# Attention and mixture of experts in one kernel: the gate's places, the masks and the first pair's halves at other steps, and the last batch's token list beside the second layer

## The chip, the cores and the metric

One core of a Trainium2 chip runs the whole kernel. The metric is the device time of one launch in microseconds, lower is better; several runs of one kernel are shown by their median.

## The reference, cut to what matters

Clustered attention feeds a mixture of experts. B, H, S, D are 4, 8, 768, 64; there are 16 clusters, 3072 tokens of width 512, 8 experts with a hidden width of 1024, and each token goes to 2 experts.

```python
q_assign = argmax(einsum('bhsd,hcd->bhsc', q_n, c_n)); k_assign = the same of k_n
mask = q_assign[..., :, None] == k_assign[..., None, :]
attn = softmax(where(mask, q @ k.T / sqrt(D), -1e9))
x = (attn @ v) as [B * S, H * D]
noisy = x @ w_gate + log1p(exp(x @ w_noise)) * noise
two best experts of each token, weights by softmax over the two
out[token] += weight * (relu(x[token] @ w1[e]) @ w2[e])      # for both experts e
```

## The kernel before

**Pairs and steps.** The attention goes over 16 pairs of heads, 4 pairs to a batch, 12 steps to a pair. In step t TensorE (PE) computes the scores of one block of 128 keys (`scores`, L547), ScalarE (ACT) takes their exponent (L548), and a step later GpSimd (POOL) splits it into two halves of 16 bits (`split_p`, L559; VectorE (DVE) does it for the last pairs). Four steps later PE multiplies them by v (`values`, L580, L582, L586), and DVE divides by the sums (L591 to L594).

**The list of steps.** All else is put by hand on thirds of steps with `at(step, function)`: a step has three slots, ahead of its scores, behind them, and behind the values. The slots fix each engine's order of instructions and the order of SP's queue, which issues nearly all DMAs; every engine works through its own order and waits where something is missing. What is put on one slot runs in the order in which the loop over the pairs put it there. In the loop `w = 12 * (p - 2)` is a pair's origin, `z = w + 36 + L` (L is 4) that of a finished batch's gate; at the end of the list `z` is 192, the last step of the attention.

**A pair's preparation.** q and k are transposed and split (`a_split`), placed into the tiles A and B by DMA (`b_place`), and compared with the centroids (`a_sims`, `a_sum`, `a_max1` to `a_eq`). `a_mask` transposes the one-hot rows on PE (L480), which waits for DVE's `oh` (L471), ACT writes them to `mk`, and `b_mask` puts them into A by four DMAs (L488). Then `b_max` finds each row's largest score: 12 times two matmuls (L516) and two DVE reductions, one of which goes to the PSUM tile `aux` (L519). `b_neg` (L526 to L528) and `b_negT` (L533) turn the result, and a DMA puts it into B (`B<-nt`).

**v.** `load_v` fills the one tile `vt`; `v_split` reads it head by head (ACT L402, L403; POOL L404). The next `load_v` waits in SP's queue until the last head was split.

**A finished pair.** `x_hi` (ACT L645) and `x_lo` (POOL L649) split its output into `xh`, `x_put` (L654) writes this to DRAM, `x_turn` (L661) transposes it by DMA into `xt`.

**A batch's gate.** `g_halves` (L681) multiplies the four turned pairs by the gate's weights, `g_turn` (L708, L713) turns the logits. `g_gate` makes a list of small operations, nearly all on DVE over 48 values a row, with the tile `aux` as their room: the first 26 (`GP`) find the two experts (`goh`, L770), then `places` counts on PE (L777, L781) where each token goes, and the rest make each token's place and weight. `g_list` scatters them into DRAM with 12 indirect DMAs on POOL (L865).

**Into the experts.** The weights of expert 0 are loaded and their maxima taken (`max_w1` L1167, `max_w2` L1181) for the scales. `layer1` (L1246) runs hidden block by hidden block (8 of them), ACT and DVE split its output (L1126 to L1129); `layer2` (L1283) runs token tile by token tile (7 tiles), DVE scales the result (L1290, L1292), POOL scatters it (L1296). The first TA = 4 tiles of expert 0 hold tokens of the first three batches alone, so that this work can start while the last batch's gate still runs. That gate's operations stand between the blocks of layer 1. Its tokens' places are not scattered: `l_hot` builds one-hot rows (DVE L838) and entries (POOL L843, L845), `l_sum` sums them on PE (L854) into the list of the later tiles (`idx`, L857). These tiles are then gathered (`gather_x`, L1226) and turned (`turn_x`, L1237), and layer 1 goes over them (`Bs`) behind the four tiles of layer 2. The eight experts' matmuls follow one behind the other to the end.

Of the kernel before, what the change touches and what calls it, by code (L numbers as in the profile page):

```python
# [36 lines left out]
        {'v': 9.0, 'vscale': 11.667, 'am': 13.333, 'amstep': 0.333, 'vsplit': 15.0, 'vstep': 1.0}],  # L37
# [7 lines left out]
class Kernel:  # L45
# [154 lines left out]
    def attention(self, ctx):  # L200
# [14 lines left out]
        self.qk, self.vt, self.vv, self.am, self.xp, self.gx = {}, {}, {}, {}, {}, {}  # L215
# [11 lines left out]
        T = AT  # L227
        for p in range(NP):
# [15 lines left out]
            for i in range(2 if p <= NP - 4 else 0):  # L244
# [35 lines left out]
            if hp == H // 2 - 1:  # L280
# [3 lines left out]
                at(z + 10, self.g_halves, b)  # L284
                at(z + 11, self.g_turn, b)
                fs = self.g_gate(b)
                k = b == B - 2
                chain(z + 11.667, T["gstep"] / (1 + k), fs[:self.GP])
                chain(z + (17 if k else 21.333), T["gstep"] / (1 + k), fs[self.GP:])
                for j in range(2 * NJ):  # L290
                    at(z + ((20 if j < 1 else 24.667 + 0.333 * j) if k else T["list"] + 4 + T["lstep"][b] * j), self.g_list, b, j)
# [319 lines left out]
    def zero_list(self):  # L611
        nc, E = self.nc, self.E
        ti = self.gp.tile([128, self.ET, 2], I32, name="lg")
# [19 lines left out]
    def x_piece(self, p, i):  # L633
        b, c = divmod(p, self.H // 2)
        if p <= self.NP - 4:
            cs = slice(64 * i, 64 * i + 64)
            return self.xp[p][:, :, cs], self.xh[:, :, 0, cs], self.xh[:, :, 1, cs]
        return self.xp[p][:, 3 * i:3 * i + 3], self.xh[:, 3 * i:3 * i + 3, 0], self.xh[:, 3 * i:3 * i + 3, 1]

    def x_hi(self, p, i):  # L640
        if i == 0:
            pool, n = (self.pre, 1) if p <= self.NP - 4 else (self.mo, 2)
            self.xh = pool.tile([128, self.NJ, 2, 128], F16, name="xh", bufs=n)
# [7 lines left out]
    def x_put(self, p, i):  # L651
# [3 lines left out]
                               self.xh.rearrange("p j i c -> p j (i c)"))  # L655

    def x_turn(self, p):
        c = p % (self.H // 2)
        if c == 0:
            self.xhT = self.gp.tile([128, self.H // 2, self.NJ, 2, 128], F16, name="xt", bufs=1)  # L660
        self.nc.sync.dma_start_transpose(self.xhT[:, c].rearrange("p j i n -> p (j i) n"),  # L661
                                         self.xh.rearrange("p j i c -> p (j i c)"))
# [681 lines left out]
```

## Time and profile before

| what | value |
|---|---|
| median of 3 runs | 1067.44 us (1065.06 to 1067.86) |
| the profiled execution's own time | 1067.94 us |
| its span | 1066.0 us |
| busy: PE, DVE, POOL, ACT | 996.5, 671.2, 575.2, 505.9 us |
| attention ends, experts begin | about 485 us |

The span runs from the first profiled instruction to the last; the time holds 1.94 us more. An engine's busy time is that in which one of its instructions runs. A row's "idle before" is the time for which its engine had nothing to run just ahead of it, with what ended this.

### The profile page before, as it was taken

The page shows a single profiled execution, that of the slowest core. Times are in us where ns is not written, and L with a number is a line of the kernel's source. Part 1 is how long each engine was busy: PE and PEld are TensorE (multiplying, and loading weights), DVE is VectorE, ACT ScalarE, POOL GpSimd, SP SyncE. Part 2 cuts the span into 40 slices and gives each one's busy share as a digit, 9 for nine tenths or more (in the row PEclk, how much of TensorE's full clock was granted, in tenths as well). Part 3 has the DMA queues.
Part 4 walks back from the last instruction along what each step waited for, and adds up shares of the span by engine and source line. Part 5 has one row for each costly group of instructions (what it writes and reads, how often), then busy time and mean ns, then how long its engine had stood idle before and what let it go on. Part 6 is the DMA issues. An engine that isn't in the chain of part 4 may idle for free.

```text
span 1066.0 us, 21880 instructions
## 1 busy us (share of the span) xinstructions
PE 996.5 (93%) x8353; PEld 679.5 (64%) x8353; DVE 671.2 (63%) x1447; ACT 505.9 (47%) x1051; POOL 575.2 (54%) x631
## 2 busy tenths in 40 slices
PE   5789999989998999897999999999999999999994
PEld 4678899889887988784554545445455454554541
DVE  5787777787778787898555655546554565445421
ACT  3467677758674867566323514315143152331510
POOL 9168697869995999682344335244342353522211
PEclk8799999999999999999999999999999999999998
DMA  7766988678877776316296945929349288392200
GB/s 203 169 173 146 210 180 213 162 184 182 205 163 195 167 158 147 123 40 153 60 250 149 206 141 153 215 69 249 117 130 205 78 182 200 93 234 76 60 33 34
DMA packets 172878, 162.78 MB, mean 153 GB/s; under 512 B 87737, under 2 KB 151609, under 8 KB 172770
## 3 DMA queue, kind: packets, MB, share of 16 engines
q1 hardware_dynamic: 159474, 124.97, 50.2%
q0 software_dynamic: 13296, 36.38, 12.2%
q8 instruction: 67, 1.10, 0.4%
q14 instruction: 41, 0.34, 0.1%
HBM read 78.21 MB, written 26.51 MB: 98 GB/s over the span
## 4 chain that ended last, share of the span: by engine, by line
PE 71%; issue 9%; DVE 8%; POOL 5%; ACT 4%; DMA 2%; SPq 1%; POOLq 0%; DVEq 0%; ACTq 0%
PE ring L1246 22%; PE ring L1283 20%; PE ring L547 9%; PE ring L516 5%; ACT pe L548 3%; PE av L580 2%; PE av L586 2%; PE av L582 2%; DVE aux L519 2%; PE ring L435 2%; PE ring L450 1%; PE ring L414 1%; DVE mm L519 1%; PE ring L1274 1%; DMA A<-mk 1%
## 5 line engine op out<-in xcount | busy, mean ns | idle before, releaser
L559 POOL TENSOR_TENSOR pl<-pe 128x768 f16<-128x768 f32 x173 | 252.1, 1469 | 67.0 <-ACT pe L548 53.4
L1246 PE MATMUL ring<-xT,w1t 128*128 128x416 f16 (+2 forms) x1536 | 275.1, 341 | 0.1
L1283 PE MATMUL ring<-w2t,hT 128*128 128x512 f16 x1152 | 251.8, 379 | 0.0
L548 ACT ACTIVATE pe<-ring,l 128x384 f32<-128x384 f32 x384 | 201.3, 578 | 71.2 <-PE ring L547 68.5
L1246 PEld LDWEIGHTS <-w1t 128*128 128x128 f16 x1536 | 149.9, 98 | 120.1 <-issue 3.5
L1126 ACT ACTIVATE hr<-ring 128x416 f32<-128x416 f32 (+2 forms) x128 | 66.6, 520 | 275.3 <-PE ring L1246 275.2
L1283 PEld LDWEIGHTS <-hT 128*128 128x128 f16 x1152 | 112.2, 98 | 133.1
L1296 POOL DMA_INDIRECT out<-yo,idx x52 | 62.7, 1205 | 225.6 <-DVE yo L1292 113.9
L519 DVE TENSOR_REDUCE aux<-ring 128x1 f32<-128x384 f32 x192 | 107.9, 562 | 78.0 <-PE ring L516 74.6
L547 PE MATMUL ring<-A 128*128 128x384 f32 x384 | 144.5, 376 | 1.1 <-ACT pe L548 0.9
L547 PE MATMUL ring<-B 128*128 128x384 f32 x384 | 131.6, 343 | 1.8 <-DMA B<-nt 1.8
L516 PE MATMUL ring<-A 128*128 128x384 f32 x384 | 108.4, 359 | 14.1 <-ACT pe L548 3.5
L1129 DVE TENSOR_TENSOR hT<-hr,hT 128x416 f16<-128x416 f32 (+3 forms) x128 | 72.0, 566 | 77.7 <-ACT hT L1128 77.4
L1292 DVE SCALAR_TENSOR_TENSOR yo<-ring,we,xt 128x512 f32<-128x512 f32 (+1 forms) x49 | 36.7, 749 | 120.9 <-PE ring L1283 106.5
L519 DVE TENSOR_REDUCE mm<-ring 128x1 f32<-128x384 f32 x192 | 105.2, 548 | 0.3 <-PE ring L516 0.2
L1226 POOL DMA_INDIRECT xg<-xs,idx x52 | 55.5, 1068 | 84.9 <-DMA xT<-xg 73.6
L580 PE MATMUL av<-vv,pe 128*128 128x65 f16 x1152 | 98.5, 196 | 0.1
L582 PE MATMUL av<-vv,pe 128*128 128x64 f16 x1152 | 97.5, 193 | 0.0
L580 PEld LDWEIGHTS <-pe 128*128 128x128 bf16 x1152 | 80.6, 100 | 14.9 <-issue 10.8
L516 PEld LDWEIGHTS ring<-A 128*128 128x128 f32 x384 | 71.3, 193 | 25.3 <-ACT pe L548 8.8
L582 PEld LDWEIGHTS <-pe 128*128 128x128 bf16 x1152 | 79.1, 99 | 0.3
L547 PEld LDWEIGHTS ring<-A 128*128 128x128 f32 x384 | 74.5, 194 | 4.2 <-ACT pe L548 2.0
(220 smaller groups left out, 1391.1 us busy)
## 6 DMA issues: line engine op xcount, KB each, us to landing
stg<-in_moe_w SPq DMA_DIRECT2D x64, 512.0 KB
A<-hl SPq DMA_DIRECT2D x30, 384.0 KB
B<-hl SPq DMA_DIRECT2D x30, 384.0 KB
vt<-in_v SPq DMA_DIRECT2D x8, 768.0 KB
xs<-xh SPq DMA_DIRECT2D x16, 384.0 KB
out<-zt SPq DMA_DIRECT2D x12, 512.0 KB
A<-hl SPq DMA_DIRECT2D x60, 96.0 KB
B<-hl SPq DMA_DIRECT2D x30, 192.0 KB
```

What stands on the lines that cost most here:

```text
L516: nc.tensor.matmul(t, A[:, 0, s, j * 128:j * 128 + 128], A[:, 1, s, n * 384:n * 384 + 384], start=True, stop=True)
L519: nc.vector.tensor_reduce(o, t, axis=X, op=OP.max, negate=True)
L547: nc.tensor.matmul(t, M[:, 1 - qi, s, ks], M[:, qi, s, ns], start=not qi, stop=bool(qi))
L548: nc.scalar.activation(pe[:, n], t, AF.Exp, bias=self.l64[:, 0:1], scale=self.scale)
L559: (nc.vector if last else nc.gpsimd).tensor_tensor(lo, pe, hi, op=OP.subtract)
L580: nc.tensor.matmul(av[:, j, :], ph[:, js], vv[:, hh, kj, 64:129], start=(kc == 0 and j == 0), stop=False, skip_group_check=True)
L582: nc.tensor.matmul(av[:, j, :64], ph[:, js], vv[:, hh, kj, 0:64], start=False, stop=False, skip_group_check=True)
L1126: nc.scalar.activation(r[:, :n], p, AF.Relu, scale=2.0 ** -HT)
L1129: nc.vector.tensor_tensor(h1, r[:, a:b], h0, op=OP.subtract)
L1246: nc.tensor.matmul(p, self.w1t[:, wi, c, f * 128:f * 128 + 128], self.xT[e][:, c, xi, n0:n1], start=(i == 0), stop=(i == 3 * ND - 1))
L1283: nc.tensor.matmul(p, self.hT[:, hi, f, t * 128:t * 128 + 128], self.w2t[:, wi, f], start=(i == 0), stop=(i == 3 * NF - 1))
L1296: i = nc.gpsimd.indirect_dma_start(out=self.out, out_offset=bass.IndirectOffsetOnAxis(ap=en[:r], axis=0), in_=yo[:r], in_offset=None, boun ...
```

## The change

- `v_split` of the first batch's second half stands 1.667 steps apart and no longer 1.
- The first pair's output is written and turned at steps 40 and 40.333, and no longer at 22.333 and 23; its halves lie in the tile `lg`, and `zero_list` takes `gl` in its place. `x_turn` of all other pairs stands 1.333 steps earlier, a third behind `x_put`.
- From pair 3 on `a_mask` and `b_mask` stand 0.667 steps later, and the 12 `b_max` begin 0.667 steps later, 0.94 steps apart.
- `g_halves` and `g_turn` stand 2 steps earlier, and so do the gate's first operations; `places` and what follows it stand 0.667 steps earlier (for the third batch 1 step later, with its first operations spread over 6.25 steps and no longer 4.167). The lists begin 0.667 steps earlier; the third batch's first entry stands 1 step later.
- The four `max_w1` of expert 0 stand at z - 15, -14, -13, -11.667, and no longer at -21, -19.667, -13, -11.
- In the experts the last gate's `places` stand ahead of block 4 and no longer of block 3, with the rest of the gate behind blocks 4 and 5 and layer 1; `max_w2` and `w2_scale` are spread over the blocks; the last two `split_w2` stand behind layer 1. `l_hot` and `count` go behind tile 0 of layer 2, `l_sum` and the gathers behind tile 1. Tile 0 of layer 2 takes all products with the upper half of w2 first.

```diff
-        {'v': 9.0, 'vscale': 11.667, ..., 'vsplit': 15.0, 'vstep': 1.0}],
+        {'v': 9.0, 'vscale': 11.667, ..., 'vsplit': 15.0, 'vstep': 1.667}],
...
-                    at(w + 45 if p else lo + 1, self.x_put, p, i)
+                    at(w + 45 if p else 40, self.x_put, p, i)
                     if p < NP - 4:
-                        at(w + 46.667 if p else lo + 1.667, self.x_turn, p)
+                        at(w + 45.333 if p else 40.333, self.x_turn, p)
...
-                at(w + P[k], f, p)
+                at(w + P[k] + (0.667 if p > 2 and k in ("mask", "bmask") else 0), f, p)
...
-                bm, bs = (T["bmax1"], T["bstep1"]) if p == 1 else (T["bmax"], T["bstep"])
+                bm, bs = (T["bmax1"], T["bstep1"]) if p == 1 else (T["bmax"], T["bstep"]) if p == 2 else (10, 0.94)
...
-                at(z + 10, self.g_halves, b)
-                at(z + 11, self.g_turn, b)
+                at(z + 8, self.g_halves, b)
+                at(z + 9, self.g_turn, b)
                 fs = self.g_gate(b)
                 k = b == B - 2
-                chain(z + 11.667, T["gstep"] / (1 + k), fs[:self.GP])
-                chain(z + (17 if k else 21.333), T["gstep"] / (1 + k), fs[self.GP:])
+                chain(z + 9.667, 0.25 if k else T["gstep"], fs[:self.GP])
+                chain(z + (18 if k else 20.667), T["gstep"] / (1 + k), fs[self.GP:])
                 for j in range(2 * NJ):
-                    at(z + ((20 if j < 1 else 24.667 + 0.333 * j) if k else T["list"] + 4 + T["lstep"][b] * j), ...)
+                    at(z + ((21 if j < 1 else 24.667 + 0.333 * j) if k else T["list"] + 3.333 + T["lstep"][b] * j), ...)
...
-            at((z - 21, z - 19.667, z - 13, z - 11)[i], self.max_w1, 0, i)
+            at((z - 15, z - 14, z - 13, z - 11.667)[i], self.max_w1, 0, i)
...
+        emit = lambda i, j: [g() for g in fs[i:j]]
+        n1, n2 = AT["cut"]
+        n3 = self.GP
+        for f in range(NF):
+            if f == 0:
+                emit(0, n1)
+                self.max_w2(0, 1)
+            elif f == 1:
+                emit(n1, n2)
+            elif f == 2:
+                emit(n2, n3)
+                self.max_w2(0, 2)
+            elif f == 3:
+                self.max_w2(0, 3)
+            elif f == 4:
+                emit(n3, n3 + 1)
             self.layer1(0, f, [A])
+            if f < 3:
+                self.x_last(self.NP - 3 + f)
+            elif f == 4:
+                self.w2_scale(0, 0)
+                emit(n3 + 1, n3 + 8)
+            elif f == 5:
+                self.w2_scale(0, 1)
+                emit(n3 + 8, n3 + 12)
+                self.split_w2(0, 0)
+            elif f == 6:
+                self.split_w2(0, 1)
+        self.split_w2(0, 2)
+        self.split_w2(0, 3)
+        self.eff(0, 0, self.TA)
+        emit(n3 + 12, len(fs))
         for t in range(TA):
...
             self.layer2(0, t)
+            if t == 0:
+                for i in range(2):
+                    self.l_hot(i)
+                self.count()
+            elif t == 1:
+                for i in range(2):
+                    self.l_sum(i)
+                for i in range(TA, T):
+                    self.gather_x(0, i)
...
+            if (e, t) == (0, 0):
+                parts.sort(key=lambda x: x[2])
```

## Rows read from the trace of the kernel before

**Rows 1.** Waits, PE, 60 to 485 us: total us, times, longest
```profile
PE ring L480 <- DVE oh L471: 5.5, 8, 1.1
PE aux L777 <- DVE aux L519: 3.9, 2, 1.9
...
PE aux L777 <- DVE nm L528: 2.9, 1, 2.9
PE ring L516 <- DMA out<-zt: 2.0, 1, 2.0
...
PE ring L533 <- DVE nm L528: 1.8, 1, 1.8
...
PE ring L516 <- DMA A<-mk: 1.0, 1, 1.0
```

**Rows 2.** Windows: us, busy (xinstructions) by engine, granted clock, DMA share, GB/s
```profile
219.80:223.10 3.30, 3.30 (x24) 3.30 (x21) 1.05 (x4) 1.48 (x4) 0.00 (x0) 0.50 0.93 207
...
503.10:509.80 6.70, 5.04 (x25) 2.05 (x25) 5.52 (x26) 0.49 (x3) 2.62 (x3) 0.50 0.41 117
```

**Rows 3.** The gate's first operation group that PE meets, by its source line
```profile
L681 PE MATMUL ring<-xt,wgh x48: 323/326/337, 188.6 to 413.4; 128*32 128x384 f16 x48
```

**Rows 4.** Timeline, DVE, ahead of the first places: start, us, instruction
```profile
217.13 0.21 DVE L770 TENSOR_TENSOR goh<-aux,gm 128x48 bf16<-128x48 f32 x1
...
218.12 0.56 DVE L519 TENSOR_REDUCE aux<-ring 128x1 f32<-128x384 f32 x1
```

**Rows 5.** Timeline, DVE, ahead of pair 15's transpose
```profile
447.56 1.21 DVE L1167 TENSOR_REDUCE wm<-stg 128x1 f32<-128x1024 f32 x1
...
460.74 0.17 DVE L528 TENSOR_TENSOR nm<-aux,nm 128x12 fp32r<-128x12 f32 x1
```

**Rows 6.** Windows, 250 to 300 us, columns as above
```profile
250.00:300.00 50.00, 48.13 (x631) 44.48 (x630) 39.02 (x95) 35.24 (x74) 48.28 (x50) 1.00 0.79 195
```

**Rows 7.** Timeline, POOL, the last v_split of the first batch
```profile
92.44 0.90 POOL L404 TENSOR_TENSOR vv<-vt,vv 128x384 f16<-128x384 f32 x1 [0.51 <-ACT vv L403]
```

**Rows 8.** Timeline, SP, behind it
```profile
93.37 0.38 SPq L364 DMA_DIRECT2D vt<-in_v  x1
...
94.53 2.99 SPq L488 DMA_DIRECT2D A<-mk  x4
```

**Rows 9.** Timeline, PE, pair 3's first row maximum
```profile
100.76 0.63 PE L516 MATMUL ring<-A 128*128 128x384 f32 x2 [1.05 <-DMA A<-mk]
```

**Rows 10.** Timeline, SP, the last turn of the first batch
```profile
177.37 0.66 SPq L654 DMA_DIRECT2D xs<-xh  x1
182.19 0.72 SPq L488 DMA_DIRECT2D B<-nt  x1
182.96 1.48 SPq L661 DMA_TRANSPOSE xt<-xh  x1
```

**Rows 11.** Windows of 1 us, 182 to 183 and 185 to 186 us
```profile
182.00:183.00 1.00, 1.00 (x8) 1.00 (x7) 0.86 (x5) 0.58 (x2) 1.00 (x1) 1.00 0.07 22
...
185.00:186.00 1.00, 1.00 (x14) 1.00 (x10) 0.00 (x0) 1.00 (x3) 1.00 (x2) 1.00 1.15 209
```

**Rows 12.** Timeline, PE, the last batch's places
```profile
504.76 0.24 PE L777 MATMUL aux<-goh,ltri 128*128 128x48 bf16 x2 [3.84 <-DVE goh L770]
```

**Rows 13.** Lines, PE, 484 to 545 us: busy us, mean ns, idle before
```profile
L1283 PE MATMUL ring<-w2t,hT 128*128 128x512 f16 x96 | 20.9, 379 | 0.0
L854 PE MATMUL ring<-ent,hot 128*128 128x112 f32 x24 | 3.2, 278 | 0.0
```

**Rows 14.** Timeline, ACT, a half of w2
```profile
516.91 1.15 ACT L1133 ACTIVATE w2t<-stg,sw 128x1024 f16<-128x1024 f32 x1
```

**Rows 15.** Timeline, POOL, entries and gathers of the last batch
```profile
519.90 1.27 POOL L843 TENSOR_TENSOR ent<-lg,tokn 128x168 f32<-128x168 f32 x1 [7.20 <-PE ring L854]
...
524.59 1.05 POOL L1226 DMA_INDIRECT xg<-xs,idx  x1 [2.14 <-DVE lsw L858]
```

**Rows 16.** Timeline, SP, turns of the gathered tiles
```profile
528.09 3.97 SPq L1237 DMA_TRANSPOSE xT<-xg  x3
```

More of the change, by code (lines that the diff above doesn't have):

```diff
@@ L36 @@
     fv=[{'v': -5.0, 'vscale': 13.0, 'am': 24.333, 'amstep': 0.333, 'vsplit': 25.333, 'vstep': 2.0},
-        {'v': 9.0, 'vscale': 11.667, 'am': 13.333, 'amstep': 0.333, 'vsplit': 15.0, 'vstep': 1.0}],
+        {'v': 9.0, 'vscale': 11.667, 'am': 13.333, 'amstep': 0.333, 'vsplit': 15.0, 'vstep': 1.667}],
     thr=0.333, bmax1=14.667, bstep1=0.5)
@@ L214, in attention @@
         self.st = [dict() for _ in range(NP)]
-        self.qk, self.vt, self.vv, self.am, self.xp, self.gx = {}, {}, {}, {}, {}, {}
+        self.qk, self.vt, self.vv, self.am, self.xp, self.gx, self.xh, self.hot, self.ent, self.xT = ({} for _ in range(10))
         L = AT["L"]
@@ L612, in zero_list @@
         nc, E = self.nc, self.E
-        ti = self.gp.tile([128, self.ET, 2], I32, name="lg")
+        ti = self.gp.tile([128, self.ET, 2], I32, name="gl", bufs=1)
         nc.gpsimd.memset(ti[:, :, 0:1], self.N)
@@ L636, in x_piece @@
             cs = slice(64 * i, 64 * i + 64)
-            return self.xp[p][:, :, cs], self.xh[:, :, 0, cs], self.xh[:, :, 1, cs]
-        return self.xp[p][:, 3 * i:3 * i + 3], self.xh[:, 3 * i:3 * i + 3, 0], self.xh[:, 3 * i:3 * i + 3, 1]
+            return self.xp[p][:, :, cs], self.xh[p][:, :, 0, cs], self.xh[p][:, :, 1, cs]
+        return self.xp[p][:, 3 * i:3 * i + 3], self.xh[p][:, 3 * i:3 * i + 3, 0], self.xh[p][:, 3 * i:3 * i + 3, 1]
     def x_hi(self, p, i):
         if i == 0:
-            pool, n = (self.pre, 1) if p <= self.NP - 4 else (self.mo, 2)
-            self.xh = pool.tile([128, self.NJ, 2, 128], F16, name="xh", bufs=n)
+            pool, k, n = (self.pre, "xh", 1) if p <= self.NP - 4 else (self.mo, "xh", 2)
+            if p == 0:
+                pool, k = self.gp, "lg"
+            self.xh[p] = pool.tile([128, self.NJ, 2, 128], F16, name=k, bufs=n)
         x, hi, lo = self.x_piece(p, i)
@@ L654, in x_put @@
         self.nc.sync.dma_start(rap(self.xs, b * 128 * NJ * W + 256 * c, [[NJ * W, 128], [W, NJ], [1, 256]]),
-                               self.xh.rearrange("p j i c -> p j (i c)"))
+                               self.xh[p].rearrange("p j i c -> p j (i c)"))
     def x_turn(self, p):
-        c = p % (self.H // 2)
-        if c == 0:
-            self.xhT = self.gp.tile([128, self.H // 2, self.NJ, 2, 128], F16, name="xt", bufs=1)
+        b, c = divmod(p, self.H // 2)
+        if b not in self.xT:
+            self.xT[b] = self.xhT = self.gp.tile([128, self.H // 2, self.NJ, 2, 128], F16, name="xt", bufs=1)
         self.nc.sync.dma_start_transpose(self.xhT[:, c].rearrange("p j i n -> p (j i) n"),
-                                         self.xh.rearrange("p j i c -> p (j i c)"))
+                                         self.xh[p].rearrange("p j i c -> p (j i c)"))
     def x_last(self, p):
@@ L851, in l_sum @@
             self.lps = self.ps()[:, :2 * W]
-        ent = self.ent.rearrange("p j k a w -> p (j k) (a w)")
+        ent = self.ent[h].rearrange("p j k a w -> p (j k) (a w)")
         for i in range(NJ):
-            nc.tensor.matmul(self.lps, self.hot[:, i], ent[:, i], start=(h == 0 and i == 0), stop=(h == 1 and i == NJ - 1))
+            nc.tensor.matmul(self.lps, self.hot[h][:, i], ent[:, i], start=(h == 0 and i == 0), stop=(h == 1 and i == NJ - 1))
         if h == 1:
@@ L902, in experts @@
         self.mo = mo = ctx.enter_context(tc.tile_pool(name="mo", bufs=1, reuse_waits="tile"))
-        self.xT = {}
         self.hT = mo.tile([128, 2, NF, self.CT], F16, name="hT")
@@ L1279, in layer2 @@
         else:
-            i = 0
-            for f in range(NF):
-                for hi, wi in ((0, 0), (0, 1), (1, 0)):
-                    nc.tensor.matmul(p, self.hT[:, hi, f, t * 128:t * 128 + 128], self.w2t[:, wi, f],
-                                     start=(i == 0), stop=(i == 3 * NF - 1))
-                    i += 1
+            parts = [(f, hi, wi) for f in range(NF) for hi, wi in ((0, 0), (0, 1), (1, 0))]
+            if (e, t) == (0, 0):
+                parts.sort(key=lambda x: x[2])
+            for i, (f, hi, wi) in enumerate(parts):
+                nc.tensor.matmul(p, self.hT[:, hi, f, t * 128:t * 128 + 128], self.w2t[:, wi, f],
+                                 start=(i == 0), stop=(i == 3 * NF - 1))
         yo = self.mo.tile([128, DM], F32, name="yo", bufs=3)
```

41 lines of the change are left out of this document (6 added, 35 removed).

## The prediction

> **What bounds the kernel now.** I read the waits of PE first, because PE is busy for nearly the whole span. Over the attention [rows 1] the reader sees few waits, and most name DVE: 5.5 us in eight waits of the masks for `oh`, 3.9 us in two waits of `places` (the first two batches), 2.9 us in that of the third batch, 1.8 us in a transpose of the row maxima. Three more name transfers or the mask behind them. Then I read the granted clock [rows 2]: behind each of the four waits of 1.8 to 2.9 us for `places` and the transpose stands a stretch of some 3.3 us at 0.50, which is the lower level of 1.2 GHz (one is shown, the other three look alike). PE is busy there all the time, so each costs another 1.65 us. A wait of 2.0 us for a transfer brought no such stretch, so the clock may or may not follow at this size. The third place is the last batch's gate: PE waits 3.84 us for `goh` [rows 12], and the clock stands at 0.50 over 503.1 to 509.8, where 5.04 us of busy time is worth half [rows 2]: 2.5 us more, 6.3 us together. The rest of the experts is matmul behind matmul, and the change does not touch it. So the time that can move is the waits of PE ahead of 545 us and the clock behind them.
>
> The length of a step follows from [rows 3]: three calls of `g_halves` stand 48 steps apart, from 188.6 to 413.4 us, the last start being some 0.6 us into its call: 224.2 / 96, about 2.3 us a step.
>
> **Places of the first two batches.** PE stopped at `places` until 218.73 us. `goh` was done at 217.34, but behind it in DVE's order stood the reduction L519, which ended at 218.68 [rows 4]. Both write to or stand ahead of the tile `aux`, and the wait is for the later. With the change the gate's operations end at z + 18 in place of z + 20, so DVE has no gate work in the last 2.7 steps (6 us) ahead of `places`; the `b_max` before it is one third of a step further up in the list, but DVE is then close behind PE. I leave 0.2 us of wait each: half of the 3.9 us each, (1.95 - 0.2 + 1.65) x 2 = 6.8 us gained. Bounds: nothing, if the wait follows the reduction, and 7.2.
>
> **Places of the third batch.** The same work is spread over 6.25 steps in place of 4.2, and `places` stands a step later, 1.7 steps (3.8 us) behind the third `b_neg` that ended the wait of 2.9 us [rows 1]. I take the whole wait, the clock, and 0.7 us of smaller waits of PE for DVE in the crowded steps before: 2.9 + 1.65 + 0.7 = 5.3 us. Bounds 0 and 6.
>
> **max_w1.** Two reductions of 1.21 us [rows 5] stood in DVE's order ahead of the `b_neg` that ended at 460.91 us; DVE was busy without a break there, so without them it ends 2.4 us earlier, and the transpose's wait of 1.8 us [rows 1] goes, with its clock: 3.4 us. All four now stand behind that `b_neg`, where the row maxima are over. Bounds 0 and 3.5.
>
> **Masks.** Each of the eight waits is at most 1.1 us [rows 1]; 0.667 steps are 1.5 us, so all should go, 5.5 us. But POOL is busy 48.28 of the 50 us from 250 to 300 [rows 6], and the next batch looks alike; what PE saves inside these two stretches it waits for POOL's halves. Two of the eight lie there, so I take six of them, 4.1 us. Bounds 2 and 5.5. `b_max` moves by as much as the mask, so the transfer has the same time as before. For pair 4 the mask waited behind other transfers (2.0 us, [rows 1]); there `b_max` comes 1.5 us later and the transfers not, so 1.5 us are gained.
>
> **v_split against pair 3's mask.** This one costs. `load_v` for the second batch stands at step 15.333, and SP held it until POOL's last `v_split` at step 18 was done: POOL ends at 93.34, SP issues at 93.37, and the four transfers of pair 3's mask are queued behind it, 94.53 to 97.52 [rows 7, 8]. PE's first row maximum of pair 3 came at 100.76, after 1.05 us of wait [rows 9]: 7.4 us from the load's issue to the start. With steps of 1.667 the last `v_split` stands at step 20, two steps or 4.6 us later; ACT's work ahead of it stays the same, so I put it 4 us later: the load at 97.4, the maximum at 104.8. PE would be there 0.667 steps after its old place: 99.7 + 1.5 = 101.2, a little earlier by the waits that ACT's lighter steps save. A wait of about 4.3 us in place of 1.05, and the clock with it: 3.3 + 1.65 = 4.9 us lost. Bounds 0 (ACT and POOL get to it earlier) and 6.7.
>
> **Halves.** The turn no longer stands behind `B<-nt` but right behind the put. In the first batch the put was issued at 177.37, the turn at 182.96 [rows 10]; the DMA engines were empty from 182 to 183 and ran the turn at about 209 GB/s [rows 11], so 384 KB take about 1.9 us, and I add 0.3 us until they are seen. With the change the mask's transfers ahead of the put come 1.5 us later, so the put is through at about 183.5 and the turn at 185.7, while `g_halves` stands two steps earlier: 188.6 - 4.6 = 184.0 [rows 3]. A wait of 1.7 us. In the next two batches POOL sets the put, and the lists that hold it up begin 1.5 us earlier; I take 0.4 us each. Sum 2.5 us lost, without the clock. Bounds 0 and 8 (three waits of 1.7 us and twice the clock or so). The Trainium skill, page "DMA: Bandwidth & Descriptors", section "Latency and other measured facts", has a transposing transfer with a non-contiguous middle dimension at 261 GB/s; an estimate by that page is 1.5 us for the turn, and 2.1 in place of 2.5 us for the sum of this part; the row shows 209, and I keep it.
>
> **The first pair's put and turn** leave SP at step 22 and come at step 40, between a v load and a mask; both places have SP time to spare, so nothing; if the turn holds up pair 5's mask, up to 2 us lost.
>
> **Last batch.** `places` stands a block later, when `goh` is done: DVE has two fewer reductions of w2 ahead of it. The 6.3 us go. What comes back: layer 2 starts while the last two halves of w2 are still to be made, 1.15 us each on ACT [rows 14] behind two instructions of the last block: I count 1.1 us of wait in tile 0. `l_sum` (3.2 us, [rows 13]) is the same work, two tiles later. Its entries are eight operations on POOL, the longest 1.27 us [rows 15], now behind the scatter of tile 0 (1.05 us, like the gather of [rows 15]); they end about 1.5 us after tile 1: 1.5 us of wait. Then the gathers and turns: they began at 524.59, the three turns ended at 532.06 [rows 15, 16], and the last lands some 2 us later: 9.5 us. Before, four tiles covered that; now two, 20.9 / 2 = 10.4 us [rows 13]. I take 0.5 us. 6.3 - 1.1 - 1.5 - 0.5 = 3.2 us gained. Bounds: 2 lost (the entries late by two more, the turns by as much) and 6.
>
> **The sum.** Gains 6.8 + 5.3 + 3.4 + 4.1 + 1.5 + 3.2 = 24.3; losses 4.9 + 2.5 = 7.4; 16.9 us. The profiled execution took 1067.94 us, 1.94 over its span of 1066.0, and 0.5 over the median of the runs. 1067.94 - 16.9 = 1051.0; I say 1051.
>
> **Rivals.** (a) The losses don't come: pair 3's mask and the halves are on time. Against it speaks SP's order in [rows 8, 10]; for it, that ACT may reach the last `v_split` early. 1051 - 7 = 1044. (b) `places` still waits for the last reduction in DVE's order and the clock still falls: [rows 4] name that reduction and not `goh`. 1051 + 6.8 + 2 to 5.3 is 1060 to 1063. (c) The list is late: the gathers are waited for ahead of `Bs`, with the clock: 1051 + 3.2 + 2 = 1056. (d) Slower than before: the turns, now ahead of `B<-nt` in SP's queue, hold it up. `B<-nt` was issued 0.8 us ahead of the turn [rows 10], and the scores two steps later read it. With 1.48 us of issue and 1.9 us of transfer ahead of it, twelve pairs could wait up to 3.4 us each, 41 us; it decides from 16.9 / 12 = 1.4 us a pair. Against it: SP was free for 4 us between put and `B<-nt` [rows 10], so the turn is usually through. The Trainium skill, page "DMA: Bandwidth & Descriptors", section "Queues, rings and completion order", says that a transfer's completion mark lands only after every earlier write of that DMA engine; by that rule a late turn would hold up `B<-nt` in full. At 2 us a pair the time is 1051 + 24 = 1075. (e) Waits only move along; no difference, 1067.
>
> **How the numbers follow.** Forecast 0.55 (1046 to 1056), (a) 0.14, (b) 0.16, (c) 0.07, (d) 0.04, (e) 0.04. The range of 8 in 10 reaches to (a) and into (b): 1042 to 1061. A measurement of this kernel tells 0.3%, 3.2 us, from no change. Faster takes the first four: 0.92 less a hundredth for worse mixtures, 0.91; same 0.05; slower 0.04.
>
> **What would show it.** Right: no wait above 0.5 us at L480 and L777, the clock at full speed behind them and behind pair 15's transpose, `places` of the last batch without a wait; a new wait of 3 to 5 us of PE for pair 3's mask near 100 us, of 1 to 2 us at L681 in the first batch, and small ones in L1283's first tile and L854. Wrong: a wait of the same size for L519 at `places`; waits of L547 for `B<-nt` in many pairs; a wait at L1246 for the turned tiles behind layer 2's fourth tile.

## The result, and the profile after

Slower, where faster was forecast: 1076.32 us (median of 6 runs, 1074.61 to 1081.48) against 1067.86 (median of 6) for the kernel before; the ratio is 1.0089, with a 95% interval of 1.0065 to 1.0113. The forecast was 1051.0, with a range of 1042 to 1061. The profiled execution took 1076.06 us, 2.3 over its span of 1073.8; that of before had a span of 1066.0.

The first view is where the time arises. L547 is the scores' matmul, once in every step; this is its line in the kernel before (count, shortest, median and longest in ns, first and last start in us), and below it the same line after.

```profile
L547 PE MATMUL ring<-A x384: 333/342/669, 40.9 to 480.3; 128*128 128x384 f32 x192
```

```profile
L547 PE MATMUL ring<-A x384: 331/339/667, 41.1 to 491.4; 128*128 128x384 f32 x192
...
  DMA B<-nt: 7.4, 8
...
  DVE aux L519: 2.1, 9
```

The attention's last step starts 11.1 us later (491.4 - 480.3). What lies behind it is shorter: 1073.8 - 491.4 = 582.4 us in place of 585.7. So the last batch's part gained some 3 us, and the attention lost 11 where its terms had forecast a gain of 13.7.

The waits of PE after, from 60 to 485 us (in total, times, longest), beside [rows 1]:

```profile
PE ring L547 <- DMA B<-nt: 7.4, 8, 1.8
PE ring L516 <- ACT pe L548: 7.4, 21, 1.5
PE ring L516 <- DMA A<-mk: 4.2, 1, 4.2
...
PE ring L547 <- DVE aux L519: 2.1, 9, 0.4
PE ring L683 <- DMA xt<-xh: 1.9, 2, 1.2
PE av L580 <- DVE stg L594: 1.4, 1, 1.4
PE ring L1166 <- DVE rs L591: 1.4, 1, 1.4
...
PE ring L516 <- ACT mk L482: 1.0, 3, 0.3
PE aux L779 <- DVE nm L528: 0.7, 1, 0.7
```

The waits that the change was aimed at are gone or nearly so: nothing at L480, and `places` (now L779) waits once for 0.7 us. In their place the reader sees three things: eight waits of the scores for `B<-nt`, one of 4.2 us for pair 3's mask, and many small ones of the row maxima (L516) and the scores for ACT's exponentials and DVE's reductions. The first is rival (d)'s sign, the second was forecast, of the third the prediction says nothing. One of the eight waits for `B<-nt`, 0.46 us at 62 us, lies ahead of the first turn; the kernel before has 1.82 us there. The other seven, 7.0 us, are new.

The granted clock, by windows (columns as in [rows 2]): its only fall between 60 us and the attention's end is at the mask's wait. The other two rows are for the DMA engines during a turn, below.

```profile
103.80:110.60 6.80, 5.76 (x44) 5.47 (x45) 2.90 (x5) 2.32 (x4) 1.86 (x2) 0.50 0.16 31
...
390.00:391.00 1.00, 1.00 (x22) 0.84 (x21) 0.50 (x2) 1.00 (x3) 0.93 (x2) 1.00 1.01 286
391.00:392.00 1.00, 1.00 (x12) 1.00 (x9) 0.66 (x3) 0.61 (x2) 0.90 (x1) 1.00 1.03 266
```

SP's timeline after, near pair 3's mask and near a turn late in the third batch, beside [rows 8] and [rows 10]:

```profile
97.65 0.38 SPq L364 DMA_DIRECT2D vt<-in_v  x1
...
98.76 2.97 SPq L488 DMA_DIRECT2D A<-mk  x4
...
388.69 0.63 SPq L656 DMA_DIRECT2D xs<-xh  x1
389.36 4.46 SPq L663 DMA_TRANSPOSE xt<-xh  x1
393.93 0.73 SPq L488 DMA_DIRECT2D B<-nt  x1
```

The load of v leaves at 97.65, where 97.4 was forecast, and pair 3's first maximum comes at 104.84:

```profile
104.84 0.98 PE L516 MATMUL ring<-A 128*128 128x384 f32 x2 [4.22 <-DMA A<-mk]
```

The turn behind the put holds SP for 4.46 us, and `B<-nt` leaves only then. The DMA engines are full meanwhile, at 286 and 266 GB/s in the two windows above. All turns by their line, after, and before, where all but the first pair's stood behind `B<-nt` (count, then shortest, median and longest in ns):

```profile
L663 SPq DMA_TRANSPOSE xt<-xh x11: 2857/3076/4462, 131.7 to 417.3; - x11
...
L663 SPq DMA_TRANSPOSE xt<-lg x1: 4406/4406/4406, 150.4 to 150.4; - x1
```

```profile
L661 SPq DMA_TRANSPOSE xt<-xh x12: 1335/1488/1907, 103.9 to 407.3; - x12
```

### The profile page after: what moved, and what is told of

Same layout as the page of the kernel before. It is cut to its first block, busy times and chain, and to the rows that moved or that the text cites. A ratio compares the mean times of both kernels' runs of the same rounds, so it can differ in the third digit from the quotient of the medians.

```text
span 1073.8 us, 21887 instructions
## 1 busy us (share of the span) xinstructions
PE 999.3 (93%) x8353; PEld 672.3 (63%) x8353; DVE 669.0 (62%) x1447; ACT 506.0 (47%) x1051; POOL 576.4 (54%) x631
## 4 chain that ended last, share of the span: by engine, by line
PE 67%; issue 9%; DMA 8%; POOL 6%; DVE 3%; ACT 3%; SPq 2%; POOLq 0%; ACTq 0%; DVEq 0%
PE ring L1258 21%; PE ring L1296 20%; PE ring L547 8%; PE ring L516 5%; ACT pe L548 2%; DMA B<-nt 2%; PE av L580 2%; PE av L586 2%; PE av L582 2%; POOL pl L559 2%; PE ring L450 2%; PE ring L435 1%; DMA xt<-xh 1%; DMA qk<-in_k 1%; DMA qk<-in_q 1%
## 5 line engine op out<-in xcount | busy, mean ns | idle before, releaser
L1258 PE MATMUL ring<-xT,w1t 128*128 128x416 f16 (+2 forms) x1536 | 272.8, 339 | 0.4 <-DMA xT<-xg 0.4
L1296 PE MATMUL ring<-w2t,hT 128*128 128x512 f16 x1152 | 252.3, 379 | 0.6 <-ACT w2t L1145 0.5
L1258 PEld LDWEIGHTS <-w1t 128*128 128x128 f16 x1536 | 149.3, 98 | 119.1 <-issue 1.4
L1296 PEld LDWEIGHTS <-hT 128*128 128x128 f16 x1152 | 112.2, 98 | 134.0 <-issue 1.1
L519 DVE TENSOR_REDUCE aux<-ring 128x1 f32<-128x384 f32 x192 | 107.5, 560 | 81.7 <-PE ring L516 77.4
L547 PE MATMUL ring<-A 128*128 128x384 f32 x384 | 141.0, 367 | 5.4 <-ACT pe L548 2.9
L547 PE MATMUL ring<-B 128*128 128x384 f32 x384 | 131.5, 343 | 7.4 <-DMA B<-nt 7.4
L516 PE MATMUL ring<-A 128*128 128x384 f32 x384 | 115.7, 377 | 17.4 <-ACT pe L548 7.4
L519 DVE TENSOR_REDUCE mm<-ring 128x1 f32<-128x384 f32 x192 | 104.9, 546 | 0.0
L580 PE MATMUL av<-vv,pe 128*128 128x65 f16 x1152 | 97.7, 195 | 1.5 <-DVE stg L594 1.4
L582 PE MATMUL av<-vv,pe 128*128 128x64 f16 x1152 | 96.8, 193 | 0.0
L580 PEld LDWEIGHTS <-pe 128*128 128x128 bf16 x1152 | 80.0, 99 | 16.9 <-issue 13.9
L516 PEld LDWEIGHTS ring<-A 128*128 128x128 f32 x384 | 66.1, 195 | 29.4 <-ACT pe L548 15.4
L547 PEld LDWEIGHTS ring<-A 128*128 128x128 f32 x384 | 73.3, 191 | 17.2 <-ACT pe L548 8.5
L547 PEld LDWEIGHTS ring<-B 128*128 128x128 f32 x384 | 73.5, 191 | 10.0 <-DMA B<-nt 10.0
```

The lines of the kernel that those rows point to most:

```text
L516: nc.tensor.matmul(t, A[:, 0, s, j * 128:j * 128 + 128], A[:, 1, s, n * 384:n * 384 + 384], start=True, stop=True)
L519: nc.vector.tensor_reduce(o, t, axis=X, op=OP.max, negate=True)
L547: nc.tensor.matmul(t, M[:, 1 - qi, s, ks], M[:, qi, s, ns], start=not qi, stop=bool(qi))
L580: nc.tensor.matmul(av[:, j, :], ph[:, js], vv[:, hh, kj, 64:129], start=(kc == 0 and j == 0), stop=False, skip_group_check=True)
L582: nc.tensor.matmul(av[:, j, :64], ph[:, js], vv[:, hh, kj, 0:64], start=False, stop=False, skip_group_check=True)
L1258: nc.tensor.matmul(p, self.w1t[:, wi, c, f * 128:f * 128 + 128], self.xT[e][:, c, xi, n0:n1], start=(i == 0), stop=(i == 3 * ND - 1))
```

## The experiments

Ratios are to the kernel before, run beside the kernel in question on the same chip; it had a median of 1071.94 us beside e1 to e4, 1067.42 beside e5 to e8, 1066.4 beside e9 to e12, 1066.97 beside e13 and e14, and 1070.08 beside e15 and e16. Where a difference of two ratios is given in us, it is the difference times 1067; by the intervals such a difference is uncertain by some 2 to 4.5 us. e4, e7 and e8 are the kernel before with the part named, but with the changed kernel's tiles (`gl`, the first pair's halves in `lg`, two buffers each for `hot` and `ent`); no run has the tiles alone. The profiles of e1 to e4, e15 and e16 contain up to some 5 us of idle time of PE marked "issue" at the attention's end, which neither profile above has; there I go by the ratios. A line's number can be some lines off from one kernel to the next (the `places` are L777 before, L779 in most others).

**e1: the turns back behind `B<-nt`.** The changed kernel, the turns of all pairs but the first and each batch's last at their old step:

```diff
-                        at(w + 45.333 if p else 40.333, self.x_turn, p)
+                        at(w + (45.333 if hp == H // 2 - 1 else 46.667) if p else 40.333, self.x_turn, p)
```

> The changed kernel with x_turn back at w + 46.667, behind B<-nt, for all pairs but the first and the last of each batch (9 turns of 12 move back). Theory T (the turn right behind the put holds SP for 3.6 to 4.5 us, so B<-nt is issued late and the next pair's scores wait): the waits of L547 for B<-nt, 7.4 us in the changed kernel, fall under 2 us, and the time falls by 5 to 8 us, from 1076.3 to 1068 to 1071. Theory S (the loss lies in the row maxima's slots: set directly ahead of the next scores they make these wait for DVE through the ring of six PSUM buffers): the B<-nt waits may go, but the time falls by less than 3 us.

1077.36 us, ratio 1.0060 (1.0041 to 1.0078): 3.1 us better than the changed kernel (1.0089 - 1.0060 = 0.0029), between the two expectations, and by the intervals not quite separated from nothing. Its turns take the old time again, and of eight waits for `B<-nt` one is left, at 62 us, ahead of the first turn:

```profile
L663 SPq DMA_TRANSPOSE xt<-xh x11: 1478/1530/3086, 135.5 to 411.4; - x11
...
PE ring L547 <- DMA B<-nt: 1.8, 1, 1.8
```

So the turns cost some 3 us here (e4 shows it from the other side), and are not the whole loss.

**e2: `v_split` back.** The changed kernel with the last `v_split` at its old step:

```diff
-'vsplit': 15.0, 'vstep': 1.667}
+'vsplit': 15.0, 'vstep': 1.0}
```

> The changed kernel with v_split 1 step apart again. Theory V (pair 3's mask is queued in SP behind the v load that waits for the last v_split): PE's wait of 4.22 us at 104.8 us falls to about 1 us, the clock stays at full speed there, and the time falls by 6 to 7.5 us, to 1069 to 1070. Rival (ACT and POOL are full there, the wait only moves to another place within a pair): under 2 us.

1076.53 us, ratio 1.0035 (1.0014 to 1.0056): 5.8 us better. Pair 3's maximum waits 0.81 us, and the clock does not fall there:

```profile
100.07 0.63 PE L516 MATMUL ring<-A 128*128 128x384 f32 x2 [0.81 <-DMA A<-mk]
```

**e3: masks and row maxima back.** The changed kernel, both at their old steps:

```diff
-                at(w + P[k] + (0.667 if p > 2 and k in ("mask", "bmask") else 0), f, p)
+                at(w + P[k], f, p)
...
-... else (T["bmax"], T["bstep"]) if p == 2 else (10, 0.94)
+... else (T["bmax"], T["bstep"])
```

> The changed kernel with masks at w + 6 and row maxima from 9.333 in steps of 1 again. Theory S: each pair's steps at which the row maxima stood off the slot between scores and values get 0.2 to 0.6 us shorter, 6 to 9 us in all, against about 4 us of mask waits that come back: 1071 to 1074. Theory M (the later masks are a gain in full, as forecast): the waits of L480 for oh come back and the time rises by 4 us, to 1080. Theory T says nothing but that the B<-nt waits stay at some 7 us.

1072.71 us, ratio 1.0005 (0.9990 to 1.0021): 9.0 us better, the largest single part. The waits at L480 are back (6.6 us in eight), and yet it is faster: what the change takes away there it loses elsewhere, and more.

**e4: the kernel before, with the turns alone moved** right behind the put.

```diff
-                        at(w + 46.667 if p else lo + 1.667, self.x_turn, p)
+                        at(w + 45.333 if p else lo + 1.667, self.x_turn, p)
```

> The kernel before with one part of the change: x_turn of all pairs but the first at w + 45.333, right behind the put. Theory T: SP's turn takes 3 to 4.5 us in place of 1.5, B<-nt is late in most pairs, waits of L547 for it of 5 to 9 us in all, time 1073 to 1077. Theory S: no waits of that size, 1067 to 1069.

1076.85 us, ratio 1.0045 (1.0028 to 1.0062): 4.8 us lost by this move alone; the turns last 1.87 to 5.59 us, and the scores wait 8.0 us for `B<-nt`, in five places. The longest, 3.0 us at 62 us, lies ahead of the first turn, so 5.0 us in four are the turns'. Behind two of these four (1.92 us at 272 us, 1.87 us at 388 us) the clock stands at 0.50 for some 3.4 us.

**e5: the three back together.** The edits of e1, e2 and e3 in the changed kernel.

> The changed kernel with the three costly parts undone together: v_split 1 step apart, x_turn back behind B<-nt but for the last pair of a batch, masks and row maxima at their old steps. What stays: places and the gate's steps, max_w1, the first pair's put and turn, the last batch's list. If theories V, T and S name the whole loss, their three single effects add (about 5.8, 3.1 and 9.0 us by the ratios to the kernel before), and the time is 1.5 to 2.5% under the changed kernel and 0.6 to 1.5% under the kernel before. Rival (the losses overlap, one wait covers another): between the two kernels.

1054.96 us, ratio 0.9888 (0.9852 to 0.9923): faster than both kernels, 12 us less than the kernel before (0.0112 x 1067). Its waits from 60 to 485 us:

```profile
PE ring L480 <- DVE oh L471: 6.5, 8, 1.5
PE ring L516 <- DMA A<-mk: 3.2, 3, 1.6
PE ring L516 <- ACT pe L548: 3.1, 8, 1.5
PE aux L779 <- DVE aux L519: 3.1, 2, 1.6
PE ring L547 <- DMA B<-nt: 1.9, 1, 1.9
...
PE ring L533 <- DVE nm L528: 1.0, 1, 1.0
```

**e6: e5 with the masks later**, as in the change (the first edit of e3 not made).

> The kernel of e5 with the masks 0.667 steps later again, the row maxima where they were before. Theory M (the mask's wait is a gain of its own): the 5 to 6 us of waits of L480 for oh go and the time is 3 to 5 us under e5. Rival (the time only moves, ACT or the mask's transfer are next): within 2 us of e5, with waits of L516 for the mask's transfer or ACT in place of those of L480.

1057.97 us, ratio 0.9938 (0.9914 to 0.9962): no gain, rather a loss of up to 5 us. L480 does not wait any more, but the time is back next to it:

```profile
PE ring L516 <- ACT pe L548: 5.0, 15, 1.5
...
PE ring L683 <- DMA xt<-xh: 2.3, 2, 1.3
```

**e7: the kernel before, the row maxima one slot later** (9.667 in place of 9.333, the same spacing; `b_neg` a slot later with them).

> The kernel before, with each row maximum from pair 3 on one slot later: behind the values, directly ahead of the next scores, in place of between scores and values; spacing 1 and the masks as before, b_neg a slot later. Theory S (the slot alone costs, through the ring of six PSUM buffers): steps with a row maximum get 0.1 to 0.3 us longer, 10 to 20 us in all, with waits of L547 for DVE's L519. Rival (it is the spacing of 0.94 that costs, by setting two maxima closer): no more than 3 us.

1067.29 us, ratio 1.0005 (0.9989 to 1.0021): no difference. I took this for proof that the maxima's place within a step is free; e13 shows that it was not.

**e8: the kernel before, with the last batch's part alone.**

> The kernel before with the new order of the last batch's gate, list and second layer alone. Forecast's term: 3.2 us gained. By the changed kernel's trace (46.1 us from the gate's turn to the later tiles' layer 1, 51.5 before, and then a wait of 2.0 us at L1157 for the maxima of expert 1's w1): 3 to 4 us gained, with that wait of 2 us. Rival (the w1 loads behind the turns make it wait longer): no gain.

1064.35 us, ratio 0.9971 (0.9952 to 0.9989): 3.1 us gained.

**e9: e5 with the row maxima as in the change** (10, and 0.94 apart), the masks old.

```diff
-... else (T["bmax"], T["bstep"])
+... else (T["bmax"], T["bstep"]) if p == 2 else (10, 0.94)
```

> The kernel of e5 (places of v_split, turns and masks as before) with one thing more as in the change: the row maxima of pairs 3 and later at step 10 and 0.94 apart, in place of 9.333 and 1.0. Theory P (the parts add up): e3 lost about 9 us to masks and maxima together and e6 about 5 to the masks, so the maxima alone cost some 4 us: ratio near 0.992, with waits of B<-nt longer than e5's total of 1.9 us. Theory T (only both together cost more, since the maxima then crowd the mask's own steps): ratio within 0.15% of e5's 0.989, and B<-nt waits of about 2 us.

1060.82 us, ratio 0.9950 (0.9937 to 0.9962): 6.6 us lost on e5 by the maxima alone, and the waits for `B<-nt` stay at 1.8 us. So the loss is in the maxima and not in `B<-nt`; against e7 this was a contradiction.

**e10: e5 with the maxima of w1 at their old steps.**

```diff
-            at((z - 15, z - 14, z - 13, z - 11.667)[i], self.max_w1, 0, i)
+            at((z - 21, z - 19.667, z - 13, z - 11)[i], self.max_w1, 0, i)
```

> The kernel of e5 with the four maxima of w1 at their steps of before. The prediction's term: their move was worth 3.4 us, so this gives ratio 0.992, a wait of about 1.8 us at pair 15's transpose (L533) with the clock at 0.5 behind it. Rival: the move only exchanged that wait for those of L580 (1.4 us) and L1166 (1.4 us) that e5 shows; with the maxima back both go and L533's comes: ratio 0.988 to 0.990, no difference from e5.

1055.79 us, ratio 0.9902 (0.9887 to 0.9916): 1.5 us worse than e5, a difference that the two intervals don't separate from nothing. L533 waits 1.8 us again, and the waits of 1.4 us at L1166 and L580 are gone: the move exchanges one for the others.

**e11: e5 with expert 1's loads of w1 issued behind layer 2's first tile**, ahead of the turns of the gathered tiles.

```diff
             self.layer2(0, t)
             if t == 0:
+                for i in range(4):
+                    self.load_w1(1, i)
...
-        if 0 <= i < 4:
+        if 0 <= i < 4 and e > 1:
             self.load_w1(e, i)
```

> The kernel of e5 with expert 1's four loads of w1 issued behind layer 2's first tile, ahead of the turns of the gathered tiles on SP, not behind them. If the wait of 2.3 us at L1157 comes from the loads standing behind the turns, it goes, and the time falls by 2 us or a little more with the clock: ratio 0.986 to 0.987. Rival: the loads, now beside the gathers of the last tiles, make these late, and the wait moves to L1258: ratio as e5's 0.989 or above.

1056.45 us, ratio 0.9912 (0.9889 to 0.9936): no gain. The 2.3 us at L1157, new with the change, go; the gathered tiles come late instead (L1258 is L1260 in this kernel; 485 to 620 us). e10 has the same exchange with the loads where they were (3.2 us in two at L1258, nothing at L1157), so the order of the loads alone does not decide which of the two waits comes:

```profile
PE ring L1260 <- DMA xT<-xg: 1.8, 1, 1.8
```

**e12: e5 with the gate's steps of before** (the first three batches).

```diff
-                at(z + 8, self.g_halves, b)
-                at(z + 9, self.g_turn, b)
+                at(z + 10, self.g_halves, b)
+                at(z + 11, self.g_turn, b)
...
-                chain(z + 9.667, 0.25 if k else T["gstep"], fs[:self.GP])
-                chain(z + (18 if k else 20.667), T["gstep"] / (1 + k), fs[self.GP:])
+                chain(z + 11.667, T["gstep"] / (1 + k), fs[:self.GP])
+                chain(z + (17 if k else 21.333), T["gstep"] / (1 + k), fs[self.GP:])
```

(The starts of the lists go back too.)

> The kernel of e5 with the gate's operations of the first three batches at their steps of before (halves and turn two steps later, the first chain as before, the second ending at places as before). The prediction's terms: the places were worth 6.8 + 5.3 us and the halves' wait cost 2.5, so this loses 9.6 us on e5: ratio near 0.998, with waits of 1.9 us at places in two batches, 2.9 us in the third, and the clock at 0.5 behind each. Rival, by the progress of e5 itself (2.3 us gained over each of the first two batches' places and 2.8 us over the third's): 7.4 us, ratio near 0.996.

1067.79 us, ratio 1.0001 (0.9980 to 1.0021): 12 us lost on e5. By the trace it is 9.1 us: the last start of L547 goes from 470.2 to 479.3. The waits at `places` are those of [rows 1] again, 3.9 us in two and 2.9 in one. They are not all of it: the scores wait for `B<-nt` in two more places than in e5 (4.6 us in three, 1.9 in one in e5). The clock falls behind the first two places, but not behind the third, where the same wait brought a fall in the kernel before.

**e13 and e14: where in a step a maximum stands.** Both are e5 with other places of the row maxima of pairs 3 and later. e13 makes e7's edit there. e14 starts them as late as the change does and packs them into the same eleven steps, but puts each ahead of its step's products with v. So e14 differs from e5 in the first maximum of each pair alone (10.333 for 9.333), and from e9 in no maximum by more than 0.667 of a step: rounded to slots, nine of the change's twelve stand behind the products there:

```diff
-                        at(w + bm + bs * (6 * s + j), self.b_max, p, s, j)
+                        at(w + (max(10, 9 + 6 * s + j) + 0.333 if p > 2 else bm + bs * (6 * s + j)), self.b_max, p, s, j)
```

> The kernel of e5 with the row maxima of pairs 3 and later at 9.667 and 1.0 apart (the edit of e7, there made on the kernel before). Theory O (their place within the step costs): in e7 the maxima came behind the products with v in every step, so that in the two steps of a pair without such products of their own PE reaches the next maximum about 0.6 us before its PSUM tile is free; what this lost was given back at the places, where PE waits less after being held up. Here the places hardly wait, so only the loss is left: about 1.0 us a pair, ratio 0.997 to 1.000, with waits of the maxima (L516) for the exponentials or for the reductions L519 above e5's. Rival F (free, as e7 looked): ratio as e5's 0.989.

> The kernel of e5 with the row maxima of pairs 3 and later as late as in the change, but ahead of each step's products with v: two in step 10, at 10.333, then one a step at 11.333 to 20.333. Theory O: the place within the step is what costs, so this is within 0.3% of e5's 0.989 (the second maximum of step 10 costs a few tenths of a us a pair). Rival S (starting one step later and being packed into eleven steps is what costs, wherever in the step): as e9, 0.995.

e13: 1064.84 us, ratio 0.9976 (0.9965 to 0.9988), 9.4 us lost on e5. e14: 1052.62 us, ratio 0.9877 (0.9856 to 0.9899), nothing lost, and the fastest kernel of this study. The later start, with two maxima in one step, is free; the place within the step is what costs, 7.8 us between e9 and e14. (In e13 `b_neg` stands a slot later too; in e9, which loses as well, it does not.) PE's timeline shows how. This is e5 in two steps of one pair, the second of them a step without products with v of its own (L580, L582, L586); those of the first are left out:

```profile
357.31 0.44 PE L547 MATMUL ring<-A 128*128 128x384 f32 x1
...
358.23 0.51 PE L516 MATMUL ring<-A 128*128 128x384 f32 x2
358.58 0.78 PE L450 MATMUL ring<-csum,sm 128*128 128x64 f32 x6
...
359.74 0.42 PE L547 MATMUL ring<-A 128*128 128x384 f32 x1
...
360.53 0.51 PE L516 MATMUL ring<-A 128*128 128x384 f32 x2
360.88 0.33 PE L547 MATMUL ring<-A 128*128 128x384 f32 x1
```

The same two steps in e13:

```profile
362.06 0.34 PE L547 MATMUL ring<-A 128*128 128x384 f32 x1
...
363.76 0.34 PE L586 MATMUL av<-vv,pl 128*128 128x65 f16 x6
363.94 0.59 PE L516 MATMUL ring<-A 128*128 128x384 f32 x2
364.37 0.34 PE L547 MATMUL ring<-A 128*128 128x384 f32 x1
...
365.07 0.34 PE L516 MATMUL ring<-A 128*128 128x384 f32 x1
365.62 0.45 PE L516 MATMUL ring<-A 128*128 128x384 f32 x1 [0.21 <-ACT pe L548]
366.09 0.44 PE L547 MATMUL ring<-A 128*128 128x384 f32 x1
```

In e5 the first step's maximum stands at 358.23, and the six matmuls of L450 and the products behind it give ACT and DVE 1.2 us before the next scores. In e13 the maximum stands behind the products (363.94), and two maxima and four score matmuls follow one another directly; the ring's next tile is still being read by the exponentials, and the second step takes 1.72 us (364.37 to 366.09) in place of 1.14. The wait column shows 0.21 of these 0.58 us; the matmul's mean holds more of it. An estimate from the means below: 24 matmuls in each of 13 pairs, 34 ns longer, are 10.6 us, beside the 9.4 lost. The line of L516 from 120 to 440 us (busy us, mean ns | idle before), in e5, e13 and e14:

```profile
L516 PE MATMUL ring<-A 128*128 128x384 f32 x286 | 77.9, 346 | 4.9 <-DMA A<-mk 2.1 <-ACT pe L548 1.5 <-DVE aux L526 0.6
```

```profile
L516 PE MATMUL ring<-A 128*128 128x384 f32 x276 | 85.7, 380 | 5.8 <-DVE aux L519 2.7 <-ACT pe L548 2.5 <-DVE aux L526 0.3
```

```profile
L516 PE MATMUL ring<-A 128*128 128x384 f32 x288 | 76.2, 346 | 2.7 <-ACT pe L548 1.5 <-DVE aux L519 0.5
```

The changed kernel has the same sight, in a step of the same kind:

```profile
378.40 0.34 PE L516 MATMUL ring<-A 128*128 128x384 f32 x1
378.95 0.44 PE L516 MATMUL ring<-A 128*128 128x384 f32 x1 [0.21 <-ACT pe L548]
```

In e7 the loss was there as well, L516 at 381 ns (351 before), but PE, held up in each pair, waited less at `places` and for a transfer (2.6 us for L519 in place of 3.9, and the 2.0 us for `out<-zt` gone). And the clock, which in the kernel before falls behind the first two places and behind pair 15's transpose, stays at 1.00 there in e7: at the prediction's 1.65 us each, 5 us more. By this estimate some 8 us came back for what the maxima lost.

**e15: the changed kernel with e14's places of the maxima; e16: e14 with the masks later.**

> The changed kernel with one thing altered: the row maxima of pairs 3 and later ahead of each step's products with v, as in e14 (two at 10.333, then one a step), in place of 10 and 0.94 apart. Theory O: their place behind those products is most of what masks and maxima lost together (9 us by e3), so this gains 6 to 9 us on the changed kernel: ratio 1.000 to 1.003; the mean of a maximum (L516) falls from 371 ns to about 350. Rival M: the masks lost it, and the maxima cost little beside them: ratio 1.006 to 1.009.

> The kernel of e14 with the masks 0.667 steps later, as in the change. The prediction's term for the masks: 4.1 us gained, ratio 0.984. Rival W, by e6's trace: the wait of L480 goes and the same time comes back at the maximum of that step, which waits for the exponentials, and the first batch's halves wait 2.3 us: ratio 0.988 to 0.991.

e15: 1074.91 us, ratio 1.0044 (1.0025 to 1.0063), 4.8 us better than the changed kernel; the mean of L516 is 351 ns. e16: 1061.07 us, ratio 0.9910 (0.9892 to 0.9929), 3.5 us worse than e14. e15 came between its two expectations, e16 at the upper end of rival W: of e3's 9 us the maxima's place carries about 5 and the masks about 4.

## Why the prediction was wrong

**The steps that failed.** The first is the sentence on the row maxima, "`b_max` moves by as much as the mask, so the transfer has the same time as before". It looked at the transfer alone and costed the new places of twelve row maxima a pair at nothing. They lose 4.8 us in the changed kernel (e15), 6.6 on e5 (e9). Cause, shown by e9 and e13 against e14: most of them stand behind the products with v.

The second is the masks: 4.1 us and 1.5 us gained, in place of which they lose about 3.5 (e16; e6 by its ratio 5). The waits at L480 do go, as forecast. But PE, no longer stopped there, catches up with ACT: in the mask's new step the two matmuls of a row maximum, 0.17 us apart elsewhere, start 0.55 us apart. In e6:

```profile
366.45 0.34 PE L516 MATMUL ring<-A 128*128 128x384 f32 x1
367.00 0.44 PE L516 MATMUL ring<-A 128*128 128x384 f32 x1 [0.21 <-ACT pe L548]
```

PE waited for DVE before and waits for ACT now; all waits of L516 for the exponentials grow from 3.1 us in e5 to 5.0. The prediction had asked only where POOL was full [rows 6], and had not asked what ends last once `oh` is on time. The halves wait longer too (L683, 2.3 us in e6 and 0.5 in e5), as their put stands behind the masks' transfers on SP. That doesn't make up the loss: all waits of PE from 60 to 485 us sum to 25.8 us in e5 and 24.4 in e6, while the last scores start 2.4 us later in e6 (472.6 for 470.2). Where the rest of the masks' loss lies, no run shows.

The third is rival (d), put at 0.04 because "SP was free for 4 us between put and `B<-nt`", with the turn at 1.48 us. That duration was taken from a turn that stood behind `B<-nt`, with the DMA engines empty [rows 10, 11]. Right behind the put it holds SP for 3.08 us in the median, so the 4 us are mostly used up. And the 4 us are those of one pair. In the kernel before, `B<-nt` follows the end of the put within some 2 us in four pairs, and in two of these, at 267 and 379 us, within 0.1; behind these two stand the waits of 1.9 us in e4. The second of them:

```profile
379.32 0.58 SPq L654 DMA_DIRECT2D xs<-xh  x1
379.99 0.72 SPq L488 DMA_DIRECT2D B<-nt  x1
```

The rival's place was right, its price was not: seven waits, 7.0 us, no pair over 1.8 us where 2 us in each were assumed, and worth 3.1 us (e1) to 4.8 us (e4). It alone would not have turned the sign. As to the completion rule of the Trainium skill, page "DMA: Bandwidth & Descriptors", section "Queues, rings and completion order", which stood beside this rival: the trace shows `B<-nt` held in SP's issue, ahead of anything that rule speaks of, and no run here tells whether its mark came late as well.

The fourth, smaller, is max_w1: 3.4 us forecast, 1.5 measured in a difference that the intervals don't separate from nothing (e10). The wait at pair 15's transpose fell from 1.8 to 1.0 us in e5, but two of 1.4 us took its place, at L580 and at the scale of w1 (L1166). The prediction took it that nothing was waiting behind the later maxima; the scale's operations stand behind them in DVE's order.

**What was right.** The places of the three batches less the halves' waits: 12.1 - 2.5 = 9.6 us gained was forecast; e12 lost 12 by the ratio and 9.1 by the trace. The parts differ, so this agreement is partly luck. In e5 the first two places still wait 1.53 and 1.57 us for L519, the wait of rival (b), where 0.2 each was forecast: 0.8 us of the 3.9 went, and the clock's fall behind each. In the changed kernel they hardly wait, but there PE is held up ahead of them (with masks and maxima back, in e3, 3.6 us in three return). Against this the halves cost 0.5 us in e5, and e12 has the 2.7 us of waits for `B<-nt` that no term held. In the changed kernel the halves waited 1.9 us in two places, 2.5 in three forecast. Pair 3's mask: the load 0.25 us from the forecast time, the maximum at 104.84 for 104.8, a wait of 4.22 for 4.3, with the clock; worth 5.8 us (e2) for 4.9. The first pair's turn took 4.41 us of SP's time, and no wait for a mask follows it: nothing, as forecast. The last batch: 3.2 forecast, 3.1 measured (e8), although its small parts differ: 0.54 us in tile 0 (L1296) for 1.1, nothing at `l_sum` for 1.5, and 2.0 us that the prediction did not have, for expert 1's maxima of w1 (L1157), whose loads stand behind the turns on SP. e10 and e11 show that this one only moves along.

**The sum again**, each term with its measured price: places and halves -12.1 by e12's ratio (-9.1 by its trace), max_w1 -1.5, last batch -3.1, `v_split` +5.8, turns +3.1, masks +3.5, maxima +4.8: +0.5 us (+3.5 with the trace's figure). Measured is 0.0089 x 1067 = +9.5. With some 2 to 4.5 us of uncertainty on each price, the 6 to 9 us between may be no more than that, or losses that come only with several parts together: `v_split`, turns, masks and maxima give back 21.4 us at once (e5 against the changed kernel), one by one 5.8 + 3.1 + 9.0 = 17.9. Falls of the clock that come and go elsewhere are in the prices too: e2's trace has three, from 347, 473 and 552 us on, that the changed kernel's has not. The runs don't settle it. What they do settle is the sign: with turns, `v_split`, masks and maxima back, the rest gains 12 us (e5), in sum about what its own terms had forecast: 12.1 - 2.5 + 3.4 + 3.2 = 16.2, less the 1.9 by which max_w1 fell short and some 2 us of new waits for masks (3.2 us in three at L516, 1.0 in one before, [rows 1]).

## What to carry to other kernels

When an operation of a saturated engine is moved within a software pipeline, ask what it stood between: a matmul may be the pause in which another engine empties the buffer that the next one needs, and such a loss shows only partly in the column of waits, so measure from start to start. A wait at a named instruction is worth something only if no other engine ends just behind; and the duration of a DMA's issue holds for its place in the queue, not for the instruction. An edit that proves free in one kernel (e7) can have been paid for by a wait that the next edit removes.

## What the runs showed of the hardware

SP's issue of the same transposing transfer of 384 KB took 1.49 us in the median behind `B<-nt`, with the put long through, and 3.08 right behind the put, 4.46 and 5.59 at the longest (after, e4), and all that SP had to issue next stood still. e1 and e4 show that its place behind the put does this; that the put's packets, which fill the DMA engines meanwhile, are the cause is read from the windows and was not tried apart. A wait of PE of 4.22 us brought the clock from 1.00 to 0.50, 2.4 to 1.2 GHz, over 6.8 us; the eight waits for `B<-nt`, 1.8 us at the longest, brought no fall in the changed kernel. In e4 two such waits of 1.9 us did. Nor does the same wait at the same instruction always bring one: 2.94 us at the third batch's places brought a fall in the kernel before, 2.95 us there none in e12.
